# Decode attention with a parallel MLP on one core: another cut of the first weight load, a table loaded at the start, and a shorter TensorE program

## The chip, the cores and the metric

The kernel runs on one core of one Trainium2 chip. The metric is the device time in microseconds of one execution. The profile gives the span from the first to the last instruction of one profiled execution, and its own device time beside it.

## What is computed

The reference is one decode step of a layer in which grouped-query attention over a long cache and an MLP with ReLU run in parallel on the same normalised input. Cut to what matters:

```python
x: (1, 1, 512)                                  # float32, as everything
k_cache, v_cache: (1, 8, 65536, 128)            # 8 KV heads, 268 MB each
wq: (512, 4096)   wo: (4096, 512)   w1: (512, 1792)   w2: (1792, 512)

xn = (x - mean(x)) / sqrt(var(x) + 1e-5)
q  = (xn @ wq) as 32 heads of 128               # 4 query heads share one KV head
p  = softmax(q @ k^T * 128 ** -0.5)
y  = x + (p @ v) @ wo + relu(xn @ w1) @ w2
```

## The kernel before

**Memory.** There is one SBUF tile for each stream of data: `kt` (128 x 16384) takes wq, then the 32 chunks of the K cache, then wo; `vt` (the same size) takes the 32 chunks of the V cache; `wt` takes w1 and later w2. Neither `kt` nor `vt` is doubled. While one of them is worked on, the other one is filled.

**Queues.** All loads are issued by SP, on one queue, in an order written out by hand: the first piece of wq (line 151), x twice (lines 162 and 163: once spread over the partitions, `xT`, once as a row, `xrow`), the other two pieces of wq (line 160), w1 (line 164), the first K chunk (line 166), then V and K chunks in turn (lines 169 and 171), the last V chunk, wo in three pieces (line 177), w2 in five (line 181) and the store of the result (line 183). Ahead of each K and V load SP waits for a semaphore, `kfree` or `vfree`, that says that the tile may be overwritten. `WQ_CUTS` gives the columns of the three pieces of wq; the first one counts on the semaphore `ends`, the second on `k`, the third on `wq2`.

**The start.** ACT, PE, DVE and POOL normalise x: ACT waits for `means` (constants that POOL writes), `zero` (PSUM cleared by DVE) and `x` (the load of `xT`), then runs the activations of lines 241 to 248; the last is a square root. POOL makes `xn` of it and puts it into `qpad` (line 218) once the first piece of wq is there. ACT's functions come in sets, called tables, and ACT loads one where an activation needs a function outside the current set; line 252 asks for the table of Exp ahead of the loop.

**PE's loop.** PE runs one body (`turns`) 34 times. The part from line 308 on computes scores: `qpad` against all of `kt`, 32 matmuls in 8 rounds, into PSUM. In turn 0 this is the product with wq, in turns 1 to 32 the scores on a K chunk, in turn 33 the product with wo. DVE transposes the results (line 367). The part under `If(t > 1)` belongs to the K chunk of the turn before: it carries the maximum over partitions (lines 277 and 278), four matmuls of ones against the scaled and summed w1 (line 282), which give the hidden layer of the MLP, the 32 matmuls of the probabilities against V (line 293), and the sums of the softmax (lines 300 and 303). The matmuls of line 282 write the same result in every turn, and a loop around them repeats them `PASSES` = 3 times. They wait for `sum`, which POOL gives once, when w1 is ready (line 228).

**ACT's loop.** For each chunk ACT computes the correction of the running sums (line 255), which also gives `kfree`, and the exponentials (line 257), which with V's landing release line 293. Line 300 gives `vfree`.

**The end.** After the loop PE multiplies the hidden layer `hT` with w2: lines 332 and 329 for the first ten blocks and the product with wo, line 340 for the last four, with line 353 adding the sum of the first ten (`ysum`, made by DVE in line 414) in between, at the block where `b + 1 == W2_SUM`. At that place stands a compare-and-branch that is always taken to `done`, the next instruction (line 347; `turn` is 34 there). It carries a branch hint whose location `ahead` was marked at the top of the loop body, so the hint is an instruction that PE executes in each turn. DVE transposes the result (line 416) and SP stores it.

Of the kernel before, what the change touches and what calls it, by code (L numbers as in the profile page):

```python
# [8 lines left out]
AF = mybir.ActivationFunctionType  # L9
# [22 lines left out]
CT = 4  # L32
# [3 lines left out]
NCH = SK // CHUNK  # L36
# [1 line left out]
XA = D // P  # L38
WIDE = 4
ROUNDS = 8  # L40
WQ_CUTS = [4096, 4096, 8192]
WQ_SEMS = ["ends", "k", "wq2"]
WO_CUTS = [16, 8, 8]
W2_CUTS = [6, 4, 2, 1, 1]
W2_SUM = 12
W2_ROWS = 10
PASSES = 3


def take(e, sem, n=1):  # L50

    return e.sem_inc(sem, -n).wait_op(sem, n, "sem-ge")  # L52


def starts(cuts):
    return [sum(cuts[:i]) for i in range(len(cuts) + 1)]
# [3 lines left out]
def attention_and_mlp_kernel(  # L60
# [11 lines left out]
    nc = tc.nc  # L72
    sp, pe, dve, act, pool = nc.sync, nc.tensor, nc.vector, nc.scalar, nc.gpsimd
    scale = float(DH) ** -0.5

    def sbuf(name, *shape):
        return nc.alloc_sbuf_tensor(name, list(shape), F32).ap()
# [3 lines left out]
    def sem(name):  # L81
        if name not in sems:
            sems[name] = nc.alloc_semaphore(name)
        return sems[name]

    def after(ins, name, n=1):

        return ins.wait_op(sem(name), n, "sem-ge")
# [12 lines left out]
    ones = sbuf("ones", P, P)  # L101
# [33 lines left out]
    hrow = y4[:, : FB * 32]  # L135
# [6 lines left out]
    v_row = v[0].rearrange("(n p b) d -> n p (b d)", p=P, b=NB)  # L142
    wq_at, wo_at, w2_at = starts(WQ_CUTS), starts(WO_CUTS), starts(W2_CUTS)

# [5 lines left out]

    load = sp.dma_start(kt[:, : WQ_CUTS[0]], wq_row[:, : WQ_CUTS[0]]).then_inc(sem(WQ_SEMS[0]), 16)  # L151
    tc.no_tile_sem_insts.add(load.ins.name)
# [3 lines left out]
    inside = section.enter_context(tc.tile_critical(sync_engine=mybir.EngineType.Pool, no_gpsimd_drain=True))  # L156
    for i in range(len(WQ_CUTS)):
        cut = slice(wq_at[i], wq_at[i + 1])
# [74 lines left out]
    def next_of(ins):  # L233

        ins.then_inc(sem("act"), 1)
        take(act, sem("act"))

    act.wait_ge(sem("means"), 1)
    act.wait_ge(sem("zero"), 1)
    act.wait_ge(sem("x"), 16)  # L240
# [24 lines left out]
    hb = wt[:, :f].rearrange("p (b e) -> p b e", e=P)  # L265
# [3 lines left out]
    turn = nc.alloc_registers("turn", engines=[pe.engine])  # L269
    nc.regs_mov(turn, 0)  # L270
    nc.br("turns", engines=[pe.engine])
    with nc.body("turns", valid_engines=[pe.engine]):
        t = nc.snap(turn, min_val=0, max_val=NCH + 1)

        ahead = pe.mark_branch_hint_location()
        with pe.If(t > 1):
            after(pe.transpose(pma[:GROUP, :P], m, ident), "d2p").then_inc(sem("p2d"), 1)  # L277
            after(pe.matmul(pmb[:, :GROUP], ones[:GROUP, :], dg, start=True, stop=True), "d2p", 2).then_inc(sem("p2d"), 1)  # L278

            with pe.Fori(0, PASSES):  # L280
                for c in range(CT):
                    ins = pe.matmul(  # L282
                        hrow[32 * c : 32 * c + 1, :], ones[:, :1], hb[:, :, 32 * c : 32 * c + 32],
                        start=True, stop=True,
                    )
                    if c == 0:
                        after(ins, "sum")
            take(pe, sem("v"), 17)
            n = NB // WIDE
            for i in range(n):  # L290
                c = 32 * (i % CT)
                b = i * WIDE
                last = pe.matmul(  # L293
                    acc[c : c + WIDE * GROUP, :],
                    probs[:, b : b + WIDE, :].rearrange("p b g -> p (b g)"),
                    vt[:, b * DH : (b + WIDE) * DH],
                    start=(i < CT), stop=(i >= n - CT),
                )
            last.then_inc(sem("p2d"), 1)
            pe.matmul(lo_new[:, 0, :], ones, part_sum, start=True, stop=True).then_inc(sem("vfree"), 1)  # L300
            take(pe, sem("d2p"), 3)
            for b in range(WIDE):
                last = pe.matmul(  # L303
                    lo_new[:, 1, :], o_sb[:, b, :], sel[:, b, :],
                    start=(b == 0), stop=(b == WIDE - 1),
                )
            last.then_inc(sem("p2d"), 1)
        take(pe, sem("q"))
        take(pe, sem("k"), 16)
        for s in range(ROUNDS):  # L310
            if s == ROUNDS - 2:
                take(pe, sem("free"), ROUNDS // 2)
            for c in range(CT):
                last = pe.matmul(  # L314
                    pair[s // 2 % 2][32 * c : 32 * c + 32, s % 2 * 512 : s % 2 * 512 + 512], qpad,
                    kb[:, s * 16 : s * 16 + 16, c, :], start=True, stop=True,
                )
                if c == 0 and s % 2 == 0 and s < ROUNDS - 2:
                    after(last, "free", s // 2 + 1)
            if s % 2:  # L320
                last.then_inc(sem("p2d"), 1)
        nc.regs_alu(turn, turn, 1, op=ALU.add)
        pe.br_lt(turn, NCH + 2, on_true="turns", on_false="last")
    nc.switch_bb("last")

    for b in range(W2_ROWS):
# [4 lines left out]
        c = 32 * (b % CT)  # L331
# [6 lines left out]
    for b in range(W2_ROWS, FB):  # L338
        for c in range(CT):
            last = pe.matmul(  # L340
                yacc[32 * c : 32 * c + 1, :], hT[:, b : b + 1], wt[:, b * D + c * P : b * D + (c + 1) * P],
                start=(b == W2_ROWS), stop=(b == FB - 1),
            )
            if c == 0 and b in w2_at:
                after(last, f"w2{w2_at.index(b)}", 16)
        if b + 1 == W2_SUM:
            pe.br_lt(turn, NCH + 3, on_true="done", on_false="never").branch_hint(ahead)
            with nc.body("never", valid_engines=[pe.engine]):
                pe.nop()
                nc.br("done", engines=[pe.engine])  # L350
            nc.switch_bb("done")
            for c in range(CT):
                ins = pe.matmul(
                    yacc[32 * c : 32 * c + 1, :], ones[:, :1], ysum[:, c * P : (c + 1) * P],
                    start=False, stop=False,
                )
                if c == 0:
                    after(ins, "ysum")
# [96 lines left out]
```

## Time and profile before

| what | value |
|---|---|
| time, median of 3 runs (lowest, highest) | 1303.16 us (1303.02, 1303.45) |
| the profiled execution's own time | 1303.58 us |
| its span | 1302.0 us, 13053 instructions |
| mean granted TensorE clock | 0.760 |
| busy: PE / weight loads / DVE / ACT / POOL | 769.7 / 231.0 / 274.9 / 77.4 / 34.8 us |
| bytes from HBM | 560.99 MB |
| line 314 (scores) / line 293 (V) / line 282 (MLP's sums) on PE | 309.4 / 269.4 / 119.2 us |
| matmul records of line 282 | 768, two for each matmul |
| instruction packets among the DMA packets | 1 of 11235 |

A row of the timeline reads: start in us, duration in us, engine, line, operation, output and inputs, shapes, how many, and in brackets how long the engine had been idle before it and what ended that. A row of a table by windows reads: the window in us, its length, then for PE, the weight loads (PEld), DVE, ACT and POOL the busy time and the number of instructions, then the granted TensorE clock, the mean busy share of the 16 DMA engines and the GB/s. A share can exceed 1 in a short window, since a packet's bytes and time are put where it is recorded. A row of the list of waits reads: engine, line, what it waited for, us in total, times, longest. A row of the DMA issues: output and input, queue, count, size, median us from issue to landing.

### The profile page before, as it was taken

To read this page: it belongs to the slowest core of one execution; us is meant where nothing else is said; L and a number is where in the kernel's file an instruction comes from. 1 tells how busy PE (TensorE), PEld (TensorE's weight loads), DVE (VectorE), ACT (ScalarE), POOL (GpSimd) and SP (SyncE) were. 2 spreads that over 40 slices of the span, in tenths; PEclk is the share of its full clock that TensorE was granted. 3 is DMA by queue.
4 is the path that set the end of the run, shared out by engine and by line. 5 is a ranking of instruction groups with operands and counts; after the bars stand their busy time and mean duration, and the time that the engine had idled before them with its cause. 6 is when DMAs were issued, how large, how long until landed. Compare 5 with 4: busy or idle time off the path is not lost.

```text
span 1302.0 us, 13053 instructions
## 1 busy us (share of the span) xinstructions
PE 769.7 (59%) x5474; PEld 231.0 (18%) x5474; DVE 274.9 (21%) x466; ACT 77.4 (6%) x300; POOL 34.8 (3%) x30
## 2 busy tenths in 40 slices
PE   3365665555665655575566566466566556656667
PEld 1111111111111111121111121111111111112112
DVE  2211222211222221222221122221122221122222
ACT  1000000000000000000000000000000000000000
POOL 1900000000000000000000000000000000000000
PEclk9667876777777777877777787777787776678678
DMA  9999999999999999999999999999999999999998
GB/s 403 449 421 445 425 441 429 431 439 419 451 419 449 421 449 421 441 429 431 439 425 445 419 449 421 449 421 441 429 431 439 425 445 419 451 419 449 421 430 360
DMA packets 11235, 561.02 MB, mean 431 GB/s; under 512 B 1505, under 2 KB 1505, under 8 KB 1890
## 3 DMA queue, kind: packets, MB, share of 16 engines
q1 hardware_dynamic: 11234, 561.00, 99.7%
q8 instruction: 1, 0.02, 0.0%
HBM read 560.99 MB, written 0.00 MB: 431 GB/s over the span
## 4 chain that ended last, share of the span: by engine, by line
issue 94%; DMA 3%; POOL 2%; SPq 0%; PE 0%; DVE 0%; POOLq 0%
DMA wt<-w 3%; POOL wt L223 1%; POOL wt L226 0%; POOL wt L227 0%; POOL wt L228 0%; SPq L181 0%; SPq L160 0%; PE banks L340 0%; DVE ysb L416 0%; SPq L151 0%; SPq L162 0%; SPq L163 0%; POOL hT L230 0%; SPq L451 0%; POOLq L156 0%
## 5 line engine op out<-in xcount | busy, mean ns | idle before, releaser
L314 PE MATMUL banks<-kt,qpad 128*32 128x512 f32 x2176 | 309.4, 732 | 310.5 <-PEq L52 309.2
L293 PE MATMUL banks<-vt,probs 128*16 128x512 f32 x2048 | 269.4, 686 | 87.9 <-PEq L52 87.9
L367 DVE STREAM_TRANSPOSE tr<-banks 128x1024 f32<-128x1024 f32 x136 | 170.0, 1250 | 468.9 <-PE banks L314 466.0
L314 PEld LDWEIGHTS banks<-kt,qpad 128*32 128x32 f32 x2176 | 84.0, 131 | 508.8 <-issue 497.1
L293 PEld LDWEIGHTS banks<-vt,probs 128*16 128x16 f32 x2048 | 69.3, 107 | 301.4 <-issue 301.4
L282 PE MATMUL banks<-wt,ones 128*1 128x448 f32 x768 | 119.2, 774 | 0.0
L393 DVE COPY o_sb<-banks 128x512 f32<-128x512 f32 x32 | 22.1, 692 | 457.0 <-PE banks L293 457.0
L255 ACT ACTIVATE corr<-diff 128x8 f32<-128x8 f32 x32 | 6.7, 209 | 1179.6 <-ACTq L52 1179.6
L257 ACT ACTIVATE probs<-tr,nb_new 128x128 f32<-128x128 f32 x128 | 65.3, 520 | 0.0
L277 PE MATMUL banks<-ident,m 128*4 128x128 f32 x32 | 9.8, 307 | 79.0 <-DVE m L385 79.0
L303 PE MATMUL banks<-sel,o_sb 128*128 128x4 f32 x256 | 32.8, 252 | 18.7 <-PEq L52 18.7
L303 PEld LDWEIGHTS banks<-sel,o_sb 128*128 128x128 f32 x256 | 31.0, 191 | 20.5 <-issue 20.5
L230 POOL TENSOR_SCALAR hT<-ysum 128x14 f32<-128x14 f32 x1 | 0.3, 256 | 1218.4 <-DVE ysum L405 1218.4
L385 DVE TENSOR_REDUCE m<-tr 128x4 f32<-128x512 f32 x32 | 32.2, 1006 | 2.9
L282 PEld LDWEIGHTS banks<-wt,ones 128*1 128x1 f32 x768 | 20.1, 99 | 56.8 <-issue 56.2
L278 PE MATMUL banks<-dg,ones 4*128 4x4 f32 x64 | 14.8, 300 | 20.0 <-DVE dg L388 20.0
L257 ACT ACTIVATION_READ_ACCUMULATOR probs<-tr,nb_new 128x1 f32 x128 | 24.1, 188 | 0.0
L277 PEld LDWEIGHTS banks<-ident,m 128*4 128x4 f32 x32 | 2.6, 81 | 108.0 <-DVE m L385 108.0
L223 POOL TENSOR_SCALAR wt<-wt,xn 128x1792 f32<-128x1792 f32 x4 | 19.1, 4797 | 15.3 <-DMA wt<-w 15.3
L278 PEld LDWEIGHTS banks<-dg,ones 4*128 4x128 f32 x64 | 12.0, 233 | 27.2 <-DVE dg L388 27.2
L300 PEld LDWEIGHTS banks<-part_sum,ones 128*128 128x128 f32 x64 | 9.5, 188 | 27.2 <-issue 27.2
L396 DVE TENSOR_TENSOR lo_run<-lo_run,banks 128x8 f32<-128x8 f32 x32 | 5.2, 163 | 40.0 <-DVEq L52 40.0
(70 smaller groups left out, 92.5 us busy)
## 6 DMA issues: line engine op xcount, KB each, us to landing
kt<-wq SPq DMA_DIRECT2D x2, 2048.0 KB, 9.4
kt<-wq SPq DMA_DIRECT2D x1, 4096.0 KB, 20.8
kt<-wo SPq DMA_DIRECT2D x1, 4096.0 KB, 14.4
kt<-wo SPq DMA_DIRECT2D x2, 2048.0 KB, 21.2
wt<-w SPq DMA_DIRECT2D x1, 3584.0 KB, 28.8
wt<-w SPq DMA_DIRECT2D x1, 1536.0 KB, 11.7
wt<-w SPq DMA_DIRECT2D x1, 1024.0 KB, 13.8
kt<-k SPq DMA_DIRECT2D x32, 24.6
```

The lines of the kernel that those rows point to most:

```text
L223: last = pool.tensor_scalar_mul(w1_of[a], w1_of[a], xn[:, a : a + 1])
L257: last = act.activation(probs[:, :, g], tr[:, :, g], AF.Exp, bias=nb_new[:, g : g + 1], scale=scale, accum_out=part_sum[:, g : g + 1],)
L277: after(pe.transpose(pma[:GROUP, :P], m, ident), "d2p").then_inc(sem("p2d"), 1)
L278: after(pe.matmul(pmb[:, :GROUP], ones[:GROUP, :], dg, start=True, stop=True), "d2p", 2).then_inc(sem("p2d"), 1)
L282: ins = pe.matmul(hrow[32 * c : 32 * c + 1, :], ones[:, :1], hb[:, :, 32 * c : 32 * c + 32], start=True, stop=True,)
L293: last = pe.matmul(acc[c : c + WIDE * GROUP, :], probs[:, b : b + WIDE, :].rearrange("p b g -> p (b g)"), vt[:, b * DH : (b + WIDE) * DH], ...
L300: pe.matmul(lo_new[:, 0, :], ones, part_sum, start=True, stop=True).then_inc(sem("vfree"), 1)
L303: last = pe.matmul(lo_new[:, 1, :], o_sb[:, b, :], sel[:, b, :], start=(b == 0), stop=(b == WIDE - 1),)
L314: last = pe.matmul(pair[s // 2 % 2][32 * c : 32 * c + 32, s % 2 * 512 : s % 2 * 512 + 512], qpad, kb[:, s * 16 : s * 16 + 16, c, :], start ...
L367: ins = after(dve.transpose(tr2[:, s * 1024 : (s + 1) * 1024], pair[s % 2]), "p2d", s + 1)
L385: dve.reduce_max(m, tr.rearrange("p b i -> p i b")[:, :GROUP, :], axis=AX.X).then_inc(sem("d2p"), 1)
L393: after(dve.tensor_copy(o_sb.rearrange("p b d -> p (b d)"), acc), "p2d", 7).then_inc(sem("d2p"), 1)
```

## The change

Three edits. The first piece of wq has 6144 columns and the second 2048, where both had 4096. ACT loads the table of the square root ahead of its three waits. PE's program loses six instructions: the hint at the top of the loop body and the branch in the tail that it announced, the copy of the loop's counter, and the three that ran the loop of `PASSES` around line 282, so that the four matmuls run once a turn. The `If` around the part for V becomes a compare-and-branch written out, to the same two places.

```diff
-WQ_CUTS = [4096, 4096, 8192]
+WQ_CUTS = [6144, 2048, 8192]
 WQ_SEMS = ["ends", "k", "wq2"]
...
-PASSES = 3
...
+    act.preload_act_table(AF.Sqrt)
     act.wait_ge(sem("means"), 1)
     act.wait_ge(sem("zero"), 1)
     act.wait_ge(sem("x"), 16)
...
     with nc.body("turns", valid_engines=[pe.engine]):
-        t = nc.snap(turn, min_val=0, max_val=NCH + 1)
-
-        ahead = pe.mark_branch_hint_location()
-        with pe.If(t > 1):
+        pe.br_lt(turn, 2, on_true="scores", on_false="values")
+        with nc.body("values", valid_engines=[pe.engine]):
...
-            with pe.Fori(0, PASSES):
-                for c in range(CT):
-                    ins = pe.matmul(
-                        hrow[32 * c : 32 * c + 1, :], ones[:, :1], hb[:, :, 32 * c : 32 * c + 32],
-                        start=True, stop=True,
-                    )
-                    if c == 0:
-                        after(ins, "sum")
+            for c in range(CT):
+                ins = pe.matmul(
+                    hrow[32 * c : 32 * c + 1, :], ones[:, :1], hb[:, :, 32 * c : 32 * c + 32],
+                    start=True, stop=True,
+                )
+                if c == 0:
+                    after(ins, "sum")
             take(pe, sem("v"), 17)
...
             last.then_inc(sem("p2d"), 1)
+            nc.br("scores", engines=[pe.engine])
+        nc.switch_bb("scores")
         take(pe, sem("q"))
...
         if b + 1 == W2_SUM:
-            pe.br_lt(turn, NCH + 3, on_true="done", on_false="never").branch_hint(ahead)
-            with nc.body("never", valid_engines=[pe.engine]):
-                pe.nop()
-                nc.br("done", engines=[pe.engine])
-            nc.switch_bb("done")
             for c in range(CT):
```

## The prediction

> **What bounds the kernel now.** I read the account of DMA traffic first, then the order of events in one turn of the loop, then the two ends. The page gives the span and the traffic; the list of DMA issues gives the time from issue to landing.
>
> ```profile
> span 1302.0 us, 13053 instructions
> HBM read 560.99 MB, written 0.00 MB: 431 GB/s over the span
> kt<-k SPq DMA_DIRECT2D x32, 24.6
> vt<-v SPq DMA_DIRECT2D x32, 29.3
> ```
>
> The timeline of one turn, and the two of its rows that recur near the end and at a turn where the K load is late:
>
> ```profile
> 90.01 9.66 PE L314 MATMUL banks<-kt,qpad 128*32 128x512 f32 x64 [8.67 <-PEq L52]
> 104.89 0.33 SPq L171 DMA_DIRECT2D kt<-k  x1
> 109.36 7.06 PE L293 MATMUL banks<-vt,probs 128*16 128x512 f32 x64 [1.05 <-PEq L52]
> 116.98 0.33 SPq L169 DMA_DIRECT2D vt<-v  x1
> 128.72 9.09 PE L314 MATMUL banks<-kt,qpad 128*32 128x512 f32 x64 [10.38 <-PEq L52]
> ...
> 1111.37 0.33 SPq L171 DMA_DIRECT2D kt<-k  x1
> 1115.60 2.76 PE L293 MATMUL banks<-vt,probs 128*16 128x512 f32 x12 [0.80 <-PEq L52]
> ...
> 1227.44 0.33 SPq L171 DMA_DIRECT2D kt<-k  x1
> 1231.70 8.84 PE L293 MATMUL banks<-vt,probs 128*16 128x512 f32 x64 [0.83 <-PEq L52]
> ```
>
> A K chunk and a V chunk are 8.39 MB each. PE starts on K at 90.01, on V at 109.36, on the next K at 128.72: 19.35 and 19.36 us apart, 8.39 MB / 19.35 = 434 GB/s, and PE sits idle ahead of each. So PE waits for the data, and the data come at one even rate. What keeps the rate even is that the next load is in the queue before the one ahead of it is through: the K load of 104.89 is issued 4.5 us before PE starts on the V ahead of it, the late ones at 1111.37 and 1227.44 still 4.2 and 4.3 us; the V load of 116.98 is 11.7 us ahead. An edit on PE, DVE or ACT inside the loop costs or gains nothing until it eats these leads. The time is the start of the first transfer, a fixed number of bytes, and what follows the last byte.
>
> **The change part by part.**
>
> *The longer first piece and the early table.* Rows of the start:
>
> ```profile
> 0.73 0.39 SPq L151 DMA_DIRECT2D kt<-wq  x1
> 8.56 1.28 ACT L241 ACT_TABLE_LOAD   x1 [8.56 <-DMA xT<-x]
> 13.04 1.28 ACT L248 ACT_TABLE_LOAD   x1
> 16.86 5.27 PE L314 MATMUL banks<-kt,qpad 128*32 128x512 f32 x32 [4.30 <-PEq L52]
> 27.23 0.33 SPq L166 DMA_DIRECT2D kt<-k  x1
> 31.91 19.12 POOL L223 TENSOR_SCALAR wt<-wt,xn 128x1792 f32<-128x1792 f32 x4 [15.35 <-DMA wt<-w]
> 1.00:1.50 0.50, 0.00 (x0) 0.00 (x0) 0.17 (x1) 0.00 (x0) 0.44 (x4) 1.00 0.00 0
> 1.50:2.00 0.50, 0.00 (x0) 0.00 (x0) 0.00 (x0) 0.00 (x0) 0.37 (x2) 1.00 1.77 393
> 2.00:2.50 0.50, 0.00 (x0) 0.00 (x0) 0.39 (x1) 0.00 (x0) 0.39 (x2) 1.00 0.50 131
> 2.50:3.00 0.50, 0.00 (x0) 0.00 (x0) 0.50 (x1) 0.00 (x0) 0.42 (x6) 1.00 0.32 98
> ```
>
> The first piece grows by 2048 columns x 128 rows x 4 bytes = 1.05 MB, which at 431 GB/s is 2.43 us. The loads of x and of its row stand behind it in SP's queue, so x lands at 8.56 + 2.43 = 10.99. The table that ACT loads for 1.28 us once x is there is loaded ahead of ACT's three waits instead, where ACT has nothing else queued: the first activation moves from 8.56 + 1.28 = 9.84 to 10.99, 1.15 later. If the set loaded for Sqrt also serves Copy, Identity and Square, the second load at 13.04 goes too, 1.28 less, and PE starts at 16.86 + 1.15 - 1.28 = 16.73. Were both loads to stay, it would start 2.43 later, at 19.3. The first two pieces hold as many bytes together as before and the third starts where it did. The only thing in all this that the stream can feel is the first K load, issued at 27.23 while w1 still arrives until 31.9: a lead of 4.7 us, and a load needs about 1.0 us from issue to first bytes (issue at 0.73, bytes from the second of the four windows on). Even 2.43 us late, K comes in time. I cost this part at 0. The one thing it could win is the thin stretch from 2.0 to 3.0 us, where the DMA share is 0.50 and 0.32 as the first packets fill: at most 0.6 us, and no byte is asked for earlier than before, so I take none.
>
> *The sums once.* Rows of the tail, the slowest sort of V turn, and the clock (the row without an operation is one of the chain of waits):
>
> ```profile
> 148.07 9.63 PE L293 MATMUL banks<-vt,probs 128*16 128x512 f32 x64 [4.15 <-PEq L52]
> ...
> 1264.44 4.66 PE L282 MATMUL banks<-wt,ones 128*1 128x448 f32 x24
> 1266.10:1269.50 3.40, 3.00 (x18) 0.30 (x8) 0.00 (x0) 1.33 (x6) 0.00 (x0) 0.50 1.01 434
> 1269.50:1272.90 3.40, 2.50 (x24) 0.81 (x28) 0.00 (x0) 0.00 (x0) 0.00 (x0) 1.00 1.01 434
> 1270.40 7.06 PE L293 MATMUL banks<-vt,probs 128*16 128x512 f32 x64 [1.30 <-PEq L52]
> 1281.15 8.00 PE L314 MATMUL banks<-kt,qpad 128*32 128x512 f32 x48 [1.77 <-PEq L52]
> 1281.78 2.23 SPq L181 DMA_DIRECT2D wt<-w  x5
> 1289.90 1.25 DVE L367 STREAM_TRANSPOSE tr<-banks 128x1024 f32<-128x1024 f32 x1 [1.15 <-DMA kt<-wo]
> 1294.78 0.08 PEld L329 LDWEIGHTS banks<-yd,ones 128*1 128x1 f32 x1 [0.34 <-DVE yd L410]
> 1295.98 0.17 PEld L332 LDWEIGHTS banks<-wt,hT 128*1 128x1 f32 x8 [0.69 <-DMA wt<-w]
> 1297.89 0.40 PE L353 MATMUL banks<-ysum,ones 128*1 128x128 f32 x8
> 1298.55 0.11 PEld L340 LDWEIGHTS banks<-wt,hT 128*1 128x1 f32 x8 [0.34 <-DMA wt<-w]
> 1298.56 0.44 PE banks L340 x8
> 1299.46 0.34 SPq L183 DMA_DIRECT2D y<-ysb  x1
> ```
>
> Sixteen of 24 matmuls a turn go, some 3.1 of 4.66 us here. They stood in PE's wait for V: L282 ends at 1269.10, V's matmuls begin at 1270.40, 1.30 us later, when V is there. So nothing is won directly. What may be lost is warmth. In the window before V arrives PE is busy 3.00 of 3.40 us, nearly all with these matmuls, at a granted clock of 0.50; in the next the clock is 1.00, and the 64 matmuls take 7.06. In turns where the clock came late they take 8.84 and 9.63. [...]
>
> Inside the loop 2 to 3 us more on V eat into V's lead of 11.7 us: nothing. In the last turn I take 2.6 us (9.63 - 7.06), so the scores on wo start at 1283.75 and the loads of w2, issued at 1281.78, move to 1284.4. The stream is still busy then with wo, whose last piece DVE awaits until 1289.90, so w2 follows without a gap, and the last byte, on which the last matmuls wait at 1298.55, comes when it did. Between them there is slack: 0.75 us before the last wo piece (1289.90 against 1289.15, the end of the 48 matmuls before it) and the 0.69 that PE waits for w2's second piece at 1295.98. With these 2.6 becomes 1.16 at the sum that L353 adds at 1297.89. That sum has 0.66 until the last piece at 1298.55, so 0.5 reaches the end. A cold turn of 8.84 is only 1.8 us late, and all of it is taken up. I take +0.3 us, between 0 (as the slack takes it, or as in executions of before whose own last turn was cold) and +1.0 (a clock that comes still later, in the scores on wo too).
>
> *No announced branch, six instructions fewer.* Rows of the end: what SP waits for, and the DMA queues within 1298 to 1299 us.
>
> ```profile
> SPq L451 <- PEq L451: 1.4, 2, 1.1
> q8 instruction: 1, 0.02, 5.8%
> y<-ysb SPq DMA_DIRECT2D x1, 2.0 KB, 1.4
> ```
>
> The branch and its hint compute nothing. But the one instruction packet of the whole run moves just as PE has issued its last matmul, and SP then waits 1.1 us at the closing barrier for PE's sequencer, though PE's last matmuls ended at 1298.56 + 0.44 = 1299.00. PE seems to fetch its last few instructions there. The store hides most of it: issued at 1299.46, landed 1.4 later at 1300.86, against a span of 1302.0. With six instructions fewer those last ones may already be in. The gain is bounded by what lies between the landing and PE's answer, a few tenths; I take -0.2. If instead the fetch falls a little later, where no store hides it, it costs up to the whole time from 1299.0 to the landing and the few tenths after it: 1.9 + 0.3 = +2.2, an estimate. I stay near the small end, since the fetch then lies behind the kernel's own last instruction.
>
> The sum: 0 + 0 + 0.3 - 0.2 = +0.1 against the profiled execution's own 1303.58 us (1302.0 of span and 1.58 around it). That execution is 0.42 above the median of 1303.16, so I forecast 1303.3. About 0.2%, 2.6 us, is what a measurement of this kernel tells from no change.
>
> **The rivals.**
>
> *The fetch in every turn (slower).* A turn of the loop is about 300 PE instructions: 64 pairs of weight load and matmul on K, 64 on V and the rest. Nothing fetches them again now: one packet in 1302 us. But each turn now begins with the hint that the change removes. If it is what keeps both halves of the loop resident, each of 33 back edges will fetch a packet or two. [...] The price from rows: 5.8% of 16 engines for 1 us is 0.93 us of one engine, which carries its rows of K and V without a pause and never catches up; at the stream's pace, 16 KB by 431/16 GB/s, it is 0.61. So 33 x 0.61 = 20 us to 33 x 2 x 0.93 = 61 us, about 1323 to 1364, some 1334 for one fetch a turn at 0.93. It decides as soon as one packet a turn appears. Against it: the hint names a branch far down in the tail. 17%.
>
> *The last fetch uncovered.* +2.2 and the tail's +0.3: 1303.16 + 2.5 = 1305.7; with the tail at its bound 1306.4, past the 0.2%. 12%, a third of it past the line.
>
> *The cold V reaches the end.* +1.0, with the barrier's gain of 0.2: 1304.0. Within 0.2%. 10%.
>
> *The table is not shared.* The change would not do what it says: PE starts up to 2.43 us late on wq, and the K load's lead absorbs it. 1303.3, inside the forecast.
>
> *Faster by over 0.2%.* It would take 2.6 us, and outside the even stream there are 1.5 us before the first byte and 3.5 after the last, all but tenths of them untouched. 4%.
>
> **How the numbers follow.** Forecast 57%, cold V 10%, uncovered fetch 12%, per-turn fetch 17%, faster 4%. Within 0.2%: 57 + 10 + 8 = 75%. Slower: 17 + 4 = 21%. Faster 4%. The range from 1302.5 to 1306.4 takes in the forecast with its bounds, the cold V and the uncovered fetch, 79%; it leaves out the per-turn fetch and the faster case.
>
> **What would show it.** Right: K and V still 19.35 us apart; ACT with one table load before x lands at about 11.0; the first K load near 27.1; L282 with 256 matmuls; V matmuls in the last turn at 8 to 10 us; w2's last piece waited for at 1298.5. Wrong: more than one instruction packet, K or V further apart than 19.4, a K load issued less than 1 us before V is through, or a DMA share below 0.9 in any inner slice.

## The result and the profile after

| | before | after |
|---|---|---|
| median (lowest to highest) of 7 runs | 1303.16 us (1302.92 to 1303.91) | 1307.59 us (1305.69 to 1308.96) |
| profiled execution, span | 1303.58, 1302.0 us | 1307.59, 1304.9 us |
| matmul records on the MLP's sums | 768 | 256 |

The change makes the kernel slower, by a ratio of 1.0031 with a 95% interval from 1.0021 to 1.0041; the medians differ by 4.4 us. The runs also scatter over 3.3 us where before's scatter over 1.0.

The page of after: span and traffic.

```profile
span 1304.9 us, 11735 instructions
HBM read 560.99 MB, written 0.00 MB: 430 GB/s over the span
```

The start of after: the timeline, and the DMA queues within 20 to 22 us and within 1305 to 1309 us (columns: queue, packets, MB, share of 16 engines).

```profile
0.97 1.28 ACT L237 ACT_TABLE_LOAD   x1 [0.97 <-POOLq L155]
10.68 0.20 ACT L241 ACTIVATE xc<-xT 128x4 f32<-128x4 f32 x1 [8.42 <-DMA xT<-x]
16.42 6.04 PE L313 MATMUL banks<-kt,qpad 128*32 128x512 f32 x32 [3.04 <-PEq L51]
24.12 1.25 DVE L361 STREAM_TRANSPOSE tr<-banks 128x1024 f32<-128x1024 f32 x1 [2.67 <-DMA kt<-wq]
27.92 0.33 SPq L165 DMA_DIRECT2D kt<-k  x1
32.59 4.80 POOL L222 TENSOR_SCALAR wt<-wt,xn 128x1792 f32<-128x1792 f32 x1 [16.47 <-DMA wt<-w]
...
q8 instruction: 1, 0.02, 3.2%
...
q8 instruction: 1, 0.02, 2.0%
```

The table is loaded at 0.97 and not again until that of Exp at 14.61 (before: at 8.56, 13.04 and 15.06, 1.28 us each time), and PE starts on wq at 16.42, not 16.86: that part did what it should. The new thing is the instruction packet. Before's only one moved at 1298 us; after has one between 20 and 22 us, in the middle of the stream, and another behind the end of the span. DVE then waits for wq's last piece until 24.12, and the first K load is issued at 27.92 (before: 27.23). The same wait in before:

```profile
23.44 1.25 DVE L367 STREAM_TRANSPOSE tr<-banks 128x1024 f32<-128x1024 f32 x1 [1.71 <-DMA kt<-wq]
```

Two turns of after, K load, V's matmuls, next K's matmuls; then the same turns of before.

```profile
221.78 0.33 SPq L170 DMA_DIRECT2D kt<-k  x1
226.19 8.64 PE L290 MATMUL banks<-vt,probs 128*16 128x512 f32 x64 [3.97 <-PEq L51]
246.41 1.94 PE L313 MATMUL banks<-kt,qpad 128*32 128x512 f32 x8 [9.65 <-PEq L51]
...
300.12 0.33 SPq L170 DMA_DIRECT2D kt<-k  x1
304.46 8.76 PE L290 MATMUL banks<-vt,probs 128*16 128x512 f32 x64 [3.90 <-PEq L51]
324.26 1.08 PE L313 MATMUL banks<-kt,qpad 128*32 128x512 f32 x4 [9.12 <-PEq L51]
```

```profile
220.97 0.33 SPq L171 DMA_DIRECT2D kt<-k  x1
225.47 7.06 PE L293 MATMUL banks<-vt,probs 128*16 128x512 f32 x64 [1.07 <-PEq L52]
244.82 3.64 PE L314 MATMUL banks<-kt,qpad 128*32 128x512 f32 x16 [10.37 <-PEq L52]
...
302.88 8.76 PE L293 MATMUL banks<-vt,probs 128*16 128x512 f32 x64 [3.45 <-PEq L52]
322.22 3.64 PE L314 MATMUL banks<-kt,qpad 128*32 128x512 f32 x16 [8.66 <-PEq L52]
```

From V to the next K it is 20.22 and 19.80 us in after, 19.35 and 19.34 in before. The stream is no longer even. PE's starts do not show why: the K load of 221.78 is issued 4.4 us before PE starts on V, where before has 4.5. The landing events do: each of these loads gives sixteen, taken for one from each of the 16 DMA engines. Fifteen engines have landed wq's last piece by 22.65 us, the sixteenth at 24.00; in before it is 22.79 and 23.31. The first K chunk lands over 50.06 to 51.85 us (before: 50.13 to 51.17), and the V chunks after it over 1.56 to 2.40 us each (before: 0.92 to 1.04).

The trace's record of single packets shows that the late engine is the one that carried the instructions. The packets there fall into sixteen rows in which each packet starts as the one before it ends, so a row is taken for an engine. In one row of after, the instruction packet takes 1.02 us from 20.82, and the packet of wq behind it 1.72 us, where every other one of that size between 14 and 26 us takes 1.21. The engine is through with wq at 23.54 and not at 22.03, so the fetch cost it 1.5 us. The two other profiled kernels without a hint show the same (1.02 and 1.71; 0.98 and 1.72).

A K load is issued once PE has worked on the K chunk before it, which starts when the slowest engine has landed that chunk. So a late engine delays the issue for all, while the others are through with V early: counted to the first engine's landing of V, the leads are at least 1.81 us in after and 3.16 in before. Nine of after's 31 are under 2.6 us, none of before's, and six K chunks take longer than 19.4 us after V, 2.4 us in all.

The account of the profiled executions: the last V chunk lands at 1273.36 us, not 1270.26. Of these 3.1 us 0.7 are there at the first K chunk and 2.4 are lost at K handovers. The span is 2.9 longer. The device time outside the span is 2.69 us, not 1.58: the other 1.1. That last part comes and goes: in 3 of the 7 runs it is 2.6 to 2.7 us, in 4 of them 1.6 to 1.7.

The end of after:

```profile
1273.49 8.93 PE L290 MATMUL banks<-vt,probs 128*16 128x512 f32 x64 [6.37 <-PEq L51]
1300.98 0.40 PE L347 MATMUL banks<-ysum,ones 128*1 128x128 f32 x8
1301.62 0.10 PEld L339 LDWEIGHTS banks<-wt,hT 128*1 128x1 f32 x8 [0.31 <-DMA wt<-w]
1302.52 0.35 SPq L182 DMA_DIRECT2D y<-ysb  x1
SPq L445 <- PEq L445: 1.3, 2, 0.9
```

V runs cold in the last turn, 8.93 us at a granted clock of 0.79 against 7.06 at 1.00 in before, and still the last matmuls wait for the last w2 piece as before: the slack took it.

### The profile page after: what moved, and what is told of

The parts are those of the page before. It is cut to its first block, busy times and chain, and to the rows that moved or that the text cites. A ratio compares the mean times of both kernels' runs of the same rounds, so it can differ in the third digit from the quotient of the medians.

```text
span 1304.9 us, 11735 instructions
## 1 busy us (share of the span) xinstructions
PE 711.2 (54%) x4962; PEld 215.2 (16%) x4962; DVE 274.8 (21%) x466; ACT 74.7 (6%) x299; POOL 34.9 (3%) x30
## 4 chain that ended last, share of the span: by engine, by line
issue 94%; DMA 3%; POOL 2%; SPq 0%; PE 0%; DVE 0%; POOLq 0%
DMA wt<-w 3%; POOL wt L222 1%; POOL wt L225 0%; POOL wt L226 0%; POOL wt L227 0%; PE banks L339 0%; SPq L159 0%; SPq L180 0%; DVE ysb L410 0%; PE banks L347 0%; SPq L150 0%; SPq L161 0%; SPq L162 0%; POOL hT L229 0%; SPq L445 0%
## 5 line engine op out<-in xcount | busy, mean ns | idle before, releaser
L290 PE MATMUL banks<-vt,probs 128*16 128x512 f32 x2048 | 291.6, 733 | 167.0 <-PEq L51 167.0
L279 PE MATMUL banks<-wt,ones 128*1 128x448 f32 x256 | 38.7, 685 | 0.0
L297 PE MATMUL banks<-part_sum,ones 128*128 128x4 f32 x64 | 12.3, 263 | 0.0
```

The lines of the kernel that those rows point to most:

```text
L279: ins = pe.matmul(hrow[32 * c : 32 * c + 1, :], ones[:, :1], hb[:, :, 32 * c : 32 * c + 32], start=True, stop=True,)
L290: last = pe.matmul(acc[c : c + WIDE * GROUP, :], probs[:, b : b + WIDE, :].rearrange("p b g -> p (b g)"), vt[:, b * DH : (b + WIDE) * DH], ...
```

## The experiments

Three theories. **A**: the hint kept PE from fetching 16 KB of its program early. Without it the packet comes at about 21 us (20.82 in after, 1298.77 in before); the DMA engine that carries it lags from then on, and the K loads reach the other engines too late. **B**: the start of the change delays the first K load. **C**: V runs cold, and V loads or the tail are late. After the first four a theory **D** was set beside A: the packet costs its own time, and the rest is something on PE. The measures from each profile stand in one table after the texts. "Before" is run beside each group of kernels; the ratios are to those runs.

**The start alone.** Before with:

```diff
-WQ_CUTS = [4096, 4096, 8192]
+WQ_CUTS = [6144, 2048, 8192]
...
+    act.preload_act_table(AF.Sqrt)
     act.wait_ge(sem("means"), 1)
```

> Before with the start of the change alone (longer first piece of wq, table of Sqrt ahead of the waits); PE's program untouched. Theory A (without the hint PE fetches a page of its program at about 21 us, in the middle of the stream; the one DMA engine that carries it lags to the end, and the K loads, issued when the slowest engine is through, come too late for the others): no such packet, first K load at 27.2 us, 1303.2 within 0.4. Theory B (the start does it: x lands 2 us later, so wq's turn ends later and the first K load with it): K load at 27.9 and about 1307. Theory C (V cold): 1303.2.

1303.61 us, ratio 1.0003 (0.9994 to 1.0012); first K load at 27.15. B falls.

**The sums once alone.** Before with:

```diff
-PASSES = 3
+PASSES = 1
```

> Before with the loop around the MLP's sums run once instead of three times; hint, branch and the program's length stay. Theory A: one instruction packet, at the end as before; V's matmuls longer (290 us in all instead of 269), V's leads some 1 us shorter, and 1303.2 to 1303.7. Theory B: 1303.2. Theory C (cold V delays V loads and the tail): 1305 to 1308.

1303.26 us, ratio 1.0001 (0.9992 to 1.0010). The groups of instructions show V as cold as in after (291.6 us there; the mean granted clock of the profiled execution is 0.726, in after's 0.738, in before's 0.760):

```profile
L293 PE MATMUL banks<-vt,probs 128*16 128x512 f32 x2048 | 297.8, 746 | 157.6 <-PEq L52 157.6
```

That is 28 us more on V than before's 269.4, and none of it shows in the time. C falls.

**No hint alone.** Before with:

```diff
-        ahead = pe.mark_branch_hint_location()
...
-            pe.br_lt(turn, NCH + 3, on_true="done", on_false="never").branch_hint(ahead)
-            with nc.body("never", valid_engines=[pe.engine]):
-                pe.nop()
-                nc.br("done", engines=[pe.engine])
-            nc.switch_bb("done")
```

> Before without the hint and the branch that it announces; three passes of the sums and the start stay as in before. Theory A: an instruction packet at about 21 us, one engine's last wq and w1 pieces 1.3 us behind the others, first K load at 27.9, 1305.5 to 1309 with a spread of 2 to 3 us between runs. Theories B and C: 1303.2 and no packet before 1298.

1306.50 us (1305.56 to 1310.86), ratio 1.0034 (1.0021 to 1.0048), with the packet within 15 to 27 us and the first K load where after has it:

```profile
q8 instruction: 1, 0.02, 0.5%
27.92 0.33 SPq L166 DMA_DIRECT2D kt<-k  x1
```

By the ratios the hint's removal alone makes the whole difference (after: 1.0031). By the medians it is 3.3 of the 4.4 us. The medians of the spans agree, 1304.9 us here and 1305.0 in after against 1301.6 in before; the rest is time outside the span, 1.6 to 2.0 us in the five runs here. (The passes and the start are as in before, so only two of the six instructions are gone.)

**After with the hint.** After with the two removed places put back, the hint ahead of the compare-and-branch at the head of the loop:

```diff
+        ahead = pe.mark_branch_hint_location()
         pe.br_lt(turn, 2, on_true="scores", on_false="values")
...
+            pe.br_lt(turn, NCH + 3, on_true="done", on_false="never").branch_hint(ahead)
...
```

> After with the hint and its branch put back: all else as changed. Theory A: no packet at 21 us, first K load at 27.1 to 27.2, K leads as in before, 1302.8 to 1303.5 (0.1 to 0.2 below before if PE no longer has to fetch its last instructions at the closing barrier). Theories B and C: about 1307, as after.

1303.44 us (1302.91 to 1304.28), ratio 1.0002 (0.9993 to 1.0011); no packet before 1298 us. All but 0.2 of the 4.4 us are back, with the cold V and the changed start still in; the gain hoped for at the end is not there.

**One more packet.** Before, PE untouched, with a load on one engine:

```diff
+            if i == 2:
+                sp.dma_start(extra, k[0, 0, 0:1, :4096]).then_inc(sem("extra"), 16)
...
```

> Before with one more load of 16 KB onto one partition, queued by SP just ahead of the third piece of wq and used by nobody; PE's program, hint included, is before's. It puts what the instruction packet cost one DMA engine into before without any fetch. Theory A (the engine's lag and the late K loads are the cost): first K load 0.5 to 0.8 us later than 27.2, K landing over 1.6 to 1.9 us from the first engine to the last, K leads 0.7 us shorter, losses at several K handovers, 1305 to 1308. Theory D (the packet costs its own time, 0.6 to 1.0 us, and the rest comes from PE): 1303.8 to 1304.2.

1303.58 us, ratio 1.0003 (0.9994 to 1.0012). A miss: the first K chunk landed over 0.66 us, less than in before's profile (1.04). The dose was too small. All 16 KB packets of data took 0.61 us here and none behind them was longer, so the load cost its engine 0.6 us, not the 1.5 of the 16 KB of instructions. By about 0.5 us the engines differ anyway (0.52 in the first K landing of the sums once alone), so this does not decide between A and D. The two with more bytes below do.

**After with early K loads.** The semaphore for the next K load comes from DVE, as soon as PE has read the old chunk, and not from ACT's correction:

```diff
-            turn_scores()
+            turn_scores(free="kfree")
...
-        act.activation(corr, ..., AF.Exp).then_inc(sem("kfree"), 1)
+        act.activation(corr, ..., AF.Exp)
```

> After with each K load issued as soon as PE has read the old chunk (DVE gives the semaphore ahead of its last transpose, as it does in turn 0) and not at ACT's correction: some 5 us earlier. No hint. Theory A: the packet at 21 us and the late first K load (27.9) stay, the K leads grow from 1.8 to 4.3 us to 6.5 to 9, no K handover loses time, and 1303.7 to 1304.3 is left, the engine's lag alone, with 1 us more in some executions outside the span. Theory D: 1306 to 1308, as after.

1305.60 us (1304.69 to 1306.50), ratio 1.0015 (1.0006 to 1.0024). Every K handover is on time now, and some 2 us of the 4.4 are gone. More is left than was expected: the first K chunk lands over 2.33 us, its last engine at 52.61, 1.4 behind before's, and the time outside the span is 1.8 to 2.9 us.

**With the hint too.** The kernel of the fourth experiment with the same early K loads.

> After with the hint and branch back and the early K load. Theory A: no packet at 21, no lag, no losses: 1302.8 to 1303.3, equal to before but with a narrower spread. This is the version meant to be the best of all. If DVE's extra instruction or another order of the loads cost something, 1303.5 or more.

1303.86 us (1303.27 to 1304.69), ratio 1.0003 (0.9994 to 1.0012). It was meant to be the best version and is not: where no lead was short (3.67 us the shortest), a longer one (8.22) won nothing. No version here beats before.

**The hint on the back edge.** After with the hint at the head of the loop, for the loop's own branch:

```diff
+        ahead = pe.mark_branch_hint_location()
         pe.br_lt(turn, 2, on_true="scores", on_false="values")
...
-        pe.br_lt(turn, NCH + 2, on_true="turns", on_false="last")
+        pe.br_lt(turn, NCH + 2, on_true="turns", on_false="last").branch_hint(ahead)
```

> After with a hint at the head of the loop again, announcing the loop's own back edge and not a branch in the tail. If any hint there keeps PE from fetching the next page when it first crosses into the second one, no packet at 21 and 1303.2. If it is the target in the second page that does it, the packet comes at 21 and the time is 1305.5 to 1309.

1304.38 us (1303.92 to 1305.46), ratio 1.0008 (0.9999 to 1.0017). The median is about 0.9 above that of the hint in the tail (1303.44), but the interval just takes in no change. No packet at 21 us, though the branch of this hint goes back to the loop's head. But the loop is left at 1290, and the packet then comes within 1292 to 1296 us, among the pieces of w2:

```profile
q8 instruction: 1, 0.02, 1.7%
1296.64 0.11 PEld L332 LDWEIGHTS banks<-wt,hT 128*1 128x1 f32 x8 [1.80 <-DMA wt<-w]
1299.18 0.10 PEld L340 LDWEIGHTS banks<-wt,hT 128*1 128x1 f32 x8 [0.36 <-DMA wt<-w]
```

The same two waits with the branch in the tail end 1.1 us earlier:

```profile
1295.50 0.17 PEld L332 LDWEIGHTS banks<-wt,hT 128*1 128x1 f32 x8 [0.69 <-DMA wt<-w]
1298.08 0.10 PEld L340 LDWEIGHTS banks<-wt,hT 128*1 128x1 f32 x8 [0.35 <-DMA wt<-w]
```

**32 KB and 64 KB on one engine.** Before, PE untouched, one row of K queued ahead of wq's last piece into `vt`, where the first V chunk overwrites it:

```diff
+            if i == 2:
+                sp.dma_start(vt[0:1, :n], k[0, 0, 0:1, :n]).then_inc(sem("extra"), 16)   # n = 8192, 16384
...
```

> Before with one more load of 32 KB in one row (so one DMA engine carries it, 1.2 us by the K packets' 27 GB/s), queued ahead of the third piece of wq into a part of vt that the first V chunk overwrites. Hint and PE's program as before. The 16 KB of the first such run vanished in the 0.5 us by which the engines differ anyway. Theory A: first K landing spread over 1.2 to 1.8 us, K leads some 0.5 us shorter, a few lost handovers, 1304 to 1306. Theory D (only a fetch by PE costs): 1303.2 to 1303.6.

> The same with 64 KB, 2.4 us on one engine. Theory A: first K landing spread over 2.3 to 2.9 us, first K load at 28.3 to 29, shortest K lead 1 to 1.8 us, losses in most K handovers, 1308 to 1315. If an engine's lag only adds at the end and the leads do not matter: 1305 to 1305.6. Theory D: 1303.2 to 1303.6.

1304.71 us (1304.09 to 1307.00), ratio 1.0011 (1.0002 to 1.0020), and 1306.89 us (1305.49 to 1314.30), ratio 1.0045 (1.0027 to 1.0063). Without an early fetch by PE, the late engine of the 64 KB kernel alone gives after's picture: time, scatter, spread and short leads. The 32 KB kernel is slower too, though no handover of its profiled execution lost time. One K handover of the 64 KB kernel, 19.82 us from V to K:

```profile
455.71 0.33 SPq L174 DMA_DIRECT2D kt<-k  x1
460.00 8.80 PE L296 MATMUL banks<-vt,probs 128*16 128x512 f32 x64 [0.86 <-PEq L52]
479.82 2.79 PE L317 MATMUL banks<-kt,qpad 128*32 128x512 f32 x12 [9.08 <-PEq L52]
```

D falls: the even, low times it asked for did not come. That the late engine is the whole cost is not shown. By the spread of the first K chunk (1.36 us for 32 KB, 2.45 for 64 KB) a straight line puts the 1.8 us of after and of no hint alone at some 2.4 us, an estimate, and their spans are 3.3 to 3.4 us longer. With single runs 3 to 9 us apart, this gap may be scatter.

**64 KB with early K loads.**

> The 64 KB load together with the early K loads of the run before (K issued when PE has read the old chunk, some 5 us sooner). Theory A: the spread stays at 2.3 to 2.9 us, the leads are 6 us and more, no handover loses time, and the lag alone is left: 1305 to 1306. If the losses do not come from the leads: as without the early loads.

1306.46 us (1305.98 to 1307.90), ratio 1.0027 (1.0017 to 1.0036). All K handovers on time and the scatter down from 8.8 to 1.9 us, but above the forecast 1305 to 1306: in the profiled execution the first K load was issued only at 30.37, when w1 was nearly through, and the first K chunk began to land 1.3 us later than in the kernel without early loads. PE's granted clock was 0.74 and 0.69 from 24 to 27 and 27 to 30 us there, 1.00 in the other, and wq's last rounds took 5.34 us instead of 3.64. So the time does not tell early from late loads here; the handovers and the scatter do.

**The hint once.** After with the branch in the tail, the hint ahead of the loop:

```diff
+    ahead = pe.mark_branch_hint_location()
     nc.br("turns", engines=[pe.engine])
```

> After with the announced branch in the tail, its hint executed once, ahead of the loop, and not in every turn. If a hint, once given, holds the fetch of the next page back until the announced branch has run, the packet comes at about 1298 and the time is 1302.9 to 1303.6, as with the hint in the loop. If the first taken branch (the loop's own) uses it up, the packet comes at about 21 us or in the first turn after, and the time is 1305.5 to 1309.

1303.74 us (1303.07 to 1304.29), ratio 1.0002 (0.9993 to 1.0011), packet at 1298.3, behind the branch at 1296.92. With one hint, at 13.04, the 34 turns passed without an instruction packet.

From the trace of each (times in us, the packets by their start; the wq column gives the landing of the 15th and 16th engine; a lead counts from the issue of a K load to the first engine's landing of the V before it; lost: what K chunks took beyond 19.35 after V, where it was over 0.07):

| kernel | instruction packet | wq's last piece | first K issued | first K lands | shortest lead | lost |
|---|---|---|---|---|---|---|
| before | 1298.8 | 22.79, 23.31 | 27.23 | 50.13 to 51.17 | 3.16 | 0 |
| after | 20.8, 1306.5 | 22.65, 24.00 | 27.92 | 50.06 to 51.85 | 1.81 | 2.4 |
| start alone | 1298.9 | 23.01, 23.23 | 27.15 | 50.18 to 51.09 | 3.01 | 0.1 |
| sums once | 1298.3 | 22.58, 22.65 | 26.57 | 49.99 to 50.51 | 3.67 | 0 |
| no hint | 20.8, 1304.7 | 22.63, 23.99 | 27.92 | 50.10 to 51.86 | 2.18 | 1.0 |
| after, hint | 1298.2 | 22.61, 22.82 | 26.74 | 50.14 to 50.67 | 3.67 | 0 |
| 16 KB | 1298.3 | 22.67, 22.97 | 26.90 | 50.17 to 50.83 | 3.60 | 0 |
| after, early K | 21.4, 1305.4 | 23.29, 24.51 | 28.43 | 50.27 to 52.61 | 6.71 | 0 |
| hint, early K | 1298.7 | 22.73, 22.87 | 26.80 | 50.07 to 50.74 | 8.22 | 0 |
| hint, back edge | 1293.3 | 22.76, 22.86 | 26.78 | 50.03 to 50.71 | 3.50 | 0 |
| 32 KB | 1299.2 | 23.20, 23.73 | 27.66 | 50.23 to 51.59 | 2.72 | 0 |
| 64 KB | 1302.0 | 22.71, 24.92 | 28.84 | 50.39 to 52.84 | 1.88 | 1.0 |
| 64 KB, early K | 1300.7 | 22.60, 24.75 | 30.37 | 51.64 to 53.13 | 7.51 | 0 |
| hint once | 1298.3 | 22.65, 22.76 | 26.69 | 50.14 to 50.63 | 3.59 | 0 |

## Why the prediction was wrong

*The bound* was right: the time is that of an even DMA stream (431 GB/s over before's span, 430 over after's), and the edits on PE's matmuls cost nothing while the leads hold (1303.26 us with the sums once alone).

*The start* at 0: right (1303.61, within noise). The working was right too: in after's profile x's activation starts at 10.68 (forecast 10.99) and PE on wq at 16.42 (16.73).

*The sums once* at +0.3: too much; alone they give +0.05 us, no difference. That V would start cold was the author's estimate; the runs bear it out: with the sums once alone its matmuls take 8.57 to 10.01 us at a granted clock of 0.70 to 0.82, in after 8.39 to 9.98 at 0.70 to 0.84, where 11 of before's 32 turns have 7.06 at 1.00. The slack that the sum listed in the tail took all of it.

*The announced branch* is the step that failed. The prediction set it down as an instruction that computes nothing, and counted only the last fetch at the barrier, -0.2. Its removal alone costs about +3.3 us (1306.50 against 1303.21). The row behind the -0.2 was misread: the packet at 1298.77 was taken for the fetch of PE's last few instructions. By its time it is the fetch that the hint held back, since it starts 1.4 us behind the announced branch (1297.39), and 1.3 to 1.8 behind it in all nine experiments that keep that branch. Without the hint the fetch comes at 21 us (20.82 in after, 20.83 with no hint alone). The row of such a packet does not name the engine whose program it carries; that it is PE's is inferred from the runs in which PE's program alone was changed (no hint alone, after with the hint).

The first rival, too, took the hint for what keeps a fetch away, but gave it the wrong count: one packet inside the stream, not one on each of 33 back edges, so not 20 to 61 us. No run shows a back edge that forces a fetch, nor which part of the loop PE holds: the 33 back edges pass with one packet in the stream in after and with no hint alone (at 20.8 us), and with none in before until 1298.8. What the runs show in place of that term is 16 KB, once, 4.4 us after PE's first scores begin at 16.42 in after.

*One packet priced at 0.6 to 0.9 us on one engine* was too low as a price and wrong as a sum. The fetch cost its engine 1.5 us, 1.0 for itself and 0.5 in the packet behind it, and wq's last piece landed there 1.35 us behind the other fifteen. And the sum had no term for what a late engine does to loads that are issued on the last landing: the late engine sets the issue, and the engines that were early go without work.

*The need of a load, "about 1.0 us from issue to first bytes"*, read at the idle start, is the second step that failed. In the full stream handovers lost up to 0.9 us at leads between 1.8 and 2.7 us, not each of them; above that one lost 0.14, at 3.43. And the leads were read from PE's starts, 4.2 to 4.5 us, which begin when the last engine has landed; from the first engine's landing they were 3.2 to 5.0. The kernel was half a microsecond from the edge (3.16 against 2.7), not three.

*The uncovered last fetch*, given up to +2.2, is there in part. All three profiled kernels without a hint have a second 16 KB instruction packet, which ends 2.94 (after), 2.19 (no hint) and 2.77 us (early K loads) behind the span; before has one of that size in all. In the same executions the time outside the span is 2.69, 1.96 and 2.57 us, each 0.2 to 0.25 less, against 1.58 in before. So that packet most likely sets the end; no run tests it. At the closing barrier SP waits 0.9 us for PE, not 1.1, and the hint kernels with the shorter program show no gain from it.

Of the four signs that were to show the forecast wrong, two came: more than one instruction packet, and K up to 20.22 us behind V. No K load was issued less than 1 us ahead of V's first landing (1.81), and no inner slice has a DMA share below 0.9.

## What to carry to other kernels

Where loads of one stream are issued on the landing of the one before, measure the lead from the first DMA engine through, not from the consumer's start, and keep it well above what a load needs in the full stream (here some 3 us, an estimate from the handovers that lost time, three times the idle figure). A little work on one engine can then cost more than itself, as 16 KB of instructions and 32 KB of data did here and 16 KB of data did not (+3.3, +1.5 and +0.1 us by the medians): look in the profile for the small queues, and at what time their packets move. An instruction that computes nothing can still set when something else moves: here the instruction packet came at 1298.8 us with the hint and at 20.8 without. Before one is taken out, ask what else it holds back.

## What was not expected of the hardware

In the profiled kernels with a hint the 16 KB instruction packet came only after the hint's branch had run for the last time: with a block in the tail as its target 1.3 to 1.8 us later (after with the hint: branch at 1296.86, packet at 1298.18), with the loop's own head 3.7 us later (back edge at 1289.66, packet at 1293.35), and with the hint given once ahead of the loop 1.4 us later (branch at 1296.92, packet at 1298.3). Without one the packet came 4.2 to 4.6 us after PE's first matmuls on wq, in all three profiled kernels of that kind (20.82, 20.83, and 21.37 with the early K loads). It cost its engine 1.5 us, where 16 KB of data cost 0.61. Why the packet behind it was slowed too, and why the second packet lengthens some executions by 1 us and others hardly, was not tried.
